# Up products of the third block on half the rows of TensorE, two side by side, with their messages between the halves

## Chip, cores and metric

One core of one Trainium2 chip runs the kernel as one program. The metric is the device time of one execution in microseconds (us); the kernel before takes 377.39 us, the median of three runs (377.11 to 377.71).

## The reference, cut to what matters

Three layers follow each other on 1536 tokens (2 batches of 768) of width 320:

```python
y = attn(q, k, v, i_gate, f_gate, o_gate)        # an mLSTM recurrence, 8 heads of 40, chunked in the kernel
x = y.transpose(0, 2, 1, 3).reshape(1536, 320)
h = maximum(maximum(x @ w1, x @ w2), x @ w3)      # w1, w2, w3: 320 x 768
x = h @ w_out                                     # 768 x 320
h = x @ w_in                                      # 320 x 2048
g = h * tanh(log1p(exp(h)))
out = g @ w_out2                                  # 2048 x 320
```

The change touches the second layer (the three "up" products and their maximum) for the last third of the tokens, the start of the third layer, and one memset of the first.

## The kernel before, in words

**Stages.** The tokens are cut into three blocks of 512. The attention of a block feeds the second layer of that block; when the second layer of the third block (block 2 in the code) is done, the third layer runs over all three blocks, to the end of the span.

**Arithmetic.** Each fp32 operand is split into a high part and a low remainder in a format that TensorE multiplies in one pass (`xh`, `xl`; `hh`, `hl`; `zh`, `zl`; `gh`, `gl`, and weights likewise). A product of width 320 then needs the row groups 0 to 127, 128 to 255 and 256 to 319. For the last 64 rows the high and the low part of the weight lie above each other in one 128-row slot, and the operand's 64 rows stand twice, so that a product on all 128 rows is 8 matmuls (line 570): high by high for three groups, low by high for two, high by low for three.

**The up products before.** `_P(blk, m, i)` makes one product `mm` of 128 columns of w1, w2 or w3 (`i`) by 512 tokens: 8 matmuls of 128 rows, one PSUM bank `m0`, `m1` or `m2` by `i`. There are 6 values of `m`, so 18 products and 144 matmuls in a block. `_Pa` does the first five matmuls of the first product. `_t(blk, m, 0)` copies the first product to SBUF on ScalarE (line 590); `_t(blk, m, 1)` and `_t(blk, m, 2)` take the maximum with the second and the third on VectorE (line 592). `_hh`, `_hl` split the result, and `_d` multiplies it with w_out into banks `m0`, `m1`, `m2`; `_e` and `_ea` empty these (lines 629 to 639).

**The order of the work.** Up to the start of the third layer the order on every engine is written out by hand in the three strings of `PLAN`: `follow` calls the steps in that order, and TensorE, VectorE, ScalarE, GpSimd and SyncE each keep it (`manual_schedule`, line 667). So an instruction that waits holds back what is behind it on its engine. A buffer or bank is given to a new tile when all users of the old one are done. The plan also holds, between the products, the steps that bring weights in: `fet` (a DMA on SyncE's queue), `sc` (two ScalarE passes), `mg` (VectorE), `rd` (ScalarE or VectorE), `cut` (VectorE or GpSimd), and `zh`, `zl`, which split the third layer's input. The third layer keeps an order by hand on TensorE alone, and its first matmuls are put between matmuls of the plan by the scheduler.

**Halves.** The third layer's products already run on 64 rows: `together` (line 705) issues two chains in turn, one on rows 0 to 63 and one on rows 64 to 127, into two banks. A product there is made of 8 matmuls on one half and 7 on the other, since the low weights by the low operand are left out. When one half adds to a bank that the other half wrote, TensorE must know that the writes have landed: `together` puts a no-op on SyncE's queue that waits for the last matmul of the first half (line 713), and the first matmul of the second half waits for it. This is what "message" means below.

**Late fetches.** Five weight tiles of the third layer (`LATE`, lines 790 to 793) are fetched after space of the second layer has come free.

**The startup.** `fe:0` writes rows 0 to 15 of `fzs` (line 207), `clear:2` zeroes all of `fzs` on VectorE after it (line 167), and `fl:0` writes rows 32 to 47 (line 218).

Of the kernel before, what the change touches and what calls it, by code (L numbers as in the profile page):

```python
# [8 lines left out]
F32 = mybir.dt.float32  # L9
# [5 lines left out]
P = 128  # L15
B, H, S, D = 2, 8, 768, 40
# [12 lines left out]
ZAT = (5, 12, 13)  # L29
LATE = {4: "i7", 6: "p4", 8: "p5", 10: "p6", 12: "p7"}  # L30
PLAN = (
# [33 lines left out]
)  # L65
HALF = P // 2
NP = KF2 // 2
# [2 lines left out]
I32 = mybir.dt.int32  # L70
# [4 lines left out]
def mlstm_moe_kernel(ctx, tc, fi0, fir, qk2, q3, nat, w13, wo1, wi2, wo2, ident, bmask, out):  # L75
    nc = tc.nc
# [10 lines left out]
    m1 = pa.enter_context(tc.tile_pool(name="m1", bufs=1))  # L87
# [7 lines left out]
    def bank(tag, name):  # L95
        return (mmp if tag[0] == "m" else pat).tile([P, 512], F32, tag=tag, name=name)
# [30 lines left out]
    m0 = mt0[:, 1:L + 1]  # L127
# [6 lines left out]
    xs = {}  # L134
    act = {}
# [3 lines left out]
    slabs = {}  # L139
# [441 lines left out]
    def _P(blk, m, i):  # L581
        products(blk, m, i, range(5, 8) if m == i == 0 else range(8))

    def top(blk, m):
        return zraw[:, m % 3, blk * XB:(blk + 1) * XB]

# [19 lines left out]
    @step  # L606
    def _d(blk, j, part):
        wo = slabs["o", -1]
        if part == 0:
            downs[blk, j] = bank(f"m{j}", f"mz{blk}_{j}")  # L610
        pv = downs[blk, j]
        for k in range(KF1 - 1) if part == 0 else (KF1 - 1,):
            hh, hl = hs[blk, k]
            if j < 2:
                hi, lo = wo[:, k, j * P:(j + 1) * P], wo[:, k, 384 + j * P:384 + (j + 1) * P]
                nc.tensor.matmul(pv, hi, hh, start=(k == 0), stop=False)  # L616
                nc.tensor.matmul(pv, lo, hh, start=False, stop=False)  # L617
                nc.tensor.matmul(pv, hi, hl, start=False, stop=(k == KF1 - 1))  # L618
            else:
                both = wo[:, k, 256:384]  # L620
                nc.tensor.matmul(pv, both, hh, start=(k == 0), stop=False)  # L621
                nc.tensor.matmul(pv, both, hl, start=False, stop=(k == KF1 - 1))  # L622
# [75 lines left out]
            return outp.tile([P, 512], F32, tag="mx" if p else f"o{i}", name=f"h2_{blk}_{m}")[:, 0:BLOCKS[blk][1]]  # L698
        return bank("m0" if p % 2 else f"m{1 + i}", f"h2_{blk}_{m}")[:, 0:BLOCKS[blk][1]]

    issued = []
    turns = {}
    behind = mybir.DependencyInfo(mybir.DependencyClass.Sync, mybir.DependencyReason.DATA)

    def together(*lanes):
        told = None
        for ops in zip(*lanes):
            for g, (out_, a, r, first, last) in enumerate(ops):
                was = turns.get(out_.tensor.name)
                wait = was and not first and len(lanes) == 2 and was[0] == (2, 1 - g) and not (seen and seen[-1] >= was[1])  # L710
                if wait:
                    seen.append(was[1])
                    told = nc.sync.nop().ins
                    tc.add_manual_dep(told, issued[was[1]].name, behind, reason="the other half of the rows has written the bank")
                mm = nc.tensor.matmul(out_, a, r, start=first, stop=last).ins  # L715
                if wait:
                    tc.add_manual_dep(mm, told.name, behind, reason="the other half of the rows has written the bank")
                turns[out_.tensor.name] = (len(lanes), g), len(issued)
                issued.append(mm)
        return told  # L720

    seen = []

    def lane(ps, w, i, g, zh, zl):
        r = slice(g * HALF, (g + 1) * HALF)
        seq = [(0, zh, 0), (2, zh, 0), (0, zl, 0), (1, zh, 1), (3, zh, 1), (1, zl, 1), (4, zh, 2)]
        if g == i:
            seq.append((4, zl, 2))
        n = len(seq)
        return [(ps, w[r, 2 * j + i], z[r, k], g == i and x == 0, g != i and x == n - 1) for x, (j, z, k) in enumerate(seq)]  # L730

    def expand(blk, p, ps, second):
        w, z = slabs["i", p], zs2[blk]
        if second:
            together(lane(ps[1], w, 1, 0, *z), lane(ps[0], w, 0, 1, *z))
        else:
            together(lane(ps[0], w, 0, 0, *z), lane(ps[1], w, 1, 1, *z))

# [48 lines left out]
    pools["pb2"] = ctx.enter_context(tc.tile_pool(name="pb2", bufs=4, reuse_waits="tile"))  # L787
    pz2 = ctx.enter_context(tc.tile_pool(name="pz2", bufs=1, reuse_waits="tile"))
    st2 = ctx.enter_context(tc.tile_pool(name="st2", bufs=1, reuse_waits="tile"))
    for item in LATE.values():  # L790
        k, g = item[0], int(item[1:])
        spare[k, g] = st2.tile([P, 640, 2], I32, tag=f"r_{item}", name=f"raw_{item}")
        act["fet"](k, g)

    def ahead(blk, m):
        if m in ZAT and blk + 1 < len(BLOCKS):
# [28 lines left out]
    with tc.manual_schedule(engines={ET.PE}):  # L825
        ps0, ps1 = pair_of(0, 0), pair_of(0, 1)
        expand(0, 0, ps0, False)
        expand(0, 1, ps1, False)
        expand(0, 0, ps0, True)
        evict(0, 0, ps0)  # L830
        expand(0, 1, ps1, True)
        evict(0, 1, ps1)
        for q in range(2, NP * len(BLOCKS)):
            turn_of(q)
        for ms in ((KF2 - 4, KF2 - 3), (KF2 - 2, KF2 - 1)):
            for j in range(4):
                for m in ms:
                    together(terms(last, m, j, slice(0, P), False, m == KF2 - 1))
                if KF2 - 1 in ms:
                    write(last, j)  # L840
# [69 lines left out]
```

## Time and profile before

| | us |
|---|---|
| median of three runs | 377.39 |
| the profiled execution | 377.48 |
| span of that execution (first to last instruction) | 375.7 |
| of it, second layer of the third block on TensorE | 159.66 to about 206 |
| of it, the 144 up matmuls of that block | 159.66 to 193.22 |
| of it, third layer | about 206 to 375.7 |

Times in the rows are us from the start of the span. PE is TensorE's matmul, PEld its weight load, DVE VectorE, ACT ScalarE, POOL GpSimd, SP SyncE, SPq its DMA queue. L574 is line 574 of the kernel. A row of the timeline gives start, length, engine, line, operation, output and input with shape, and how many instructions it merges; in brackets how long the engine was idle before and what ended that. A row that merges several back-to-back matmuls is as long as from the first one's start to the last one's end, and the next row can start before that end, since matmuls are pipelined. PEclk in a table of windows is the clock that TensorE was granted, 1.00 for 2.4 GHz and 0.50 for 1.2 GHz.

### The profile page before, as it was taken

How to read it: one execution, taken by the hardware profiler on the slowest of the kernel's cores; microseconds unless marked ns; L12 is line 12 of the kernel's file. 1: busy time of each engine (PE TensorE's matmuls, PEld its weight loads, DVE VectorE, ACT ScalarE, POOL GpSimd, SP SyncE). 2: the span in 40 equal slices, each digit the busy share in tenths (PEclk: the TensorE clock that was granted, in tenths of full speed). 3: DMA queues.
4: the chain of work that ended last, by engine and by line, in shares of the span. 5: the costliest groups of instructions: out<-in, count | busy, mean ns of one | idle time of the engine just before them, and what ended most of it. 6: DMA issues, size and time to landing. Idle time of an engine off the chain costs nothing.

```text
span 375.7 us, 7421 instructions
## 1 busy us (share of the span) xinstructions
PE 367.9 (98%) x2993; PEld 318.9 (85%) x2993; DVE 198.8 (53%) x344; ACT 175.6 (47%) x353; POOL 100.2 (27%) x111
## 2 busy tenths in 40 slices
PE   8899999999999999999999999999999999999996
PEld 4798888888888888888787899988988989989986
DVE  6879999998665854466582654422212112212112
ACT  4867866942521412473734967634334233333231
POOL 5783485665300122221540043330010110000000
PEclk9889999999999999999999999999999999999999
DMA  7876996637591210033420440000200000200001
GB/s 206 273 217 217 354 321 230 210 139 255 182 309 48 91 70 0 2 95 114 142 70 0 165 188 3 3 0 2 72 2 2 0 2 2 72 2 3 0 2 70
DMA packets 15668, 38.80 MB, mean 103 GB/s; under 512 B 1886, under 2 KB 8515, under 8 KB 15635
## 3 DMA queue, kind: packets, MB, share of 16 engines
q1 hardware_dynamic: 15635, 38.34, 30.8%
q8 instruction: 23, 0.38, 0.4%
q14 instruction: 10, 0.08, 0.1%
HBM read 36.29 MB, written 2.04 MB: 102 GB/s over the span
## 4 chain that ended last, share of the span: by engine, by line
PE 93%; DVE 3%; DMA 2%; issue 1%; ACT 1%; SPq 0%; DVEq 0%; ACTq 0%
PE mm L574 25%; PE o L715 23%; PE h L715 22%; PE it L394 6%; PE mz L618 2%; PE mz L616 2%; PE mz L617 2%; PE it L392 2%; PE sc_c L355 2%; PE sp L456 2%; PE mz L621 1%; DMA cp<-dram_c 1%; PE mz L622 1%; PE xp L425 1%; DVE dt L342 1%
## 5 line engine op out<-in xcount | busy, mean ns | idle before, releaser
L744 DVE TENSOR_TENSOR gl<-g,gh 128x512 fp32r<-128x512 f32 x48 | 34.9, 732 | 101.9 <-ACT g L743 101.9
L715 PE MATMUL o<-wo,gh 64*128 64x320 f32 (+1 forms) x736 | 85.0, 306 | 0.0
L715 PE MATMUL h<-zh,wi 64*128 64x512 f32 x480 | 75.2, 390 | 0.0
L574 PE MATMUL mm<-xh,w 128*128 128x512 f32 x270 | 72.0, 396 | 0.0
L715 PEld LDWEIGHTS o<-wo,gh 64*128 64x128 f32 (+1 forms) x736 | 65.0, 185 | 2.2 <-issue 0.4
L742 ACT ACTIVATE gh<-h 128x512 fp32r<-128x512 f32 x48 | 29.0, 604 | 77.7 <-PE h L715 77.6
L715 PE MATMUL o<-wo,gl 64*128 64x320 f32 (+1 forms) x368 | 59.3, 306 | 0.0
L574 PEld LDWEIGHTS mm<-xh,w 128*128 128x128 f32 x270 | 49.4, 188 | 10.7 <-issue 0.4
L715 PEld LDWEIGHTS h<-zh,wi 64*128 64x128 f32 x480 | 44.0, 185 | 9.3 <-ACT zraw L629 0.5
L715 PE MATMUL h<-zl,wi 64*128 64x512 f32 x240 | 47.3, 391 | 0.0
L574 PE MATMUL mm<-xl,w 128*128 128x512 f32 x162 | 45.7, 390 | 0.1
L574 PEld LDWEIGHTS mm<-xl,w 128*128 128x128 f32 x162 | 30.3, 188 | 6.8 <-issue 0.5
L715 PEld LDWEIGHTS o<-wo,gl 64*128 64x128 f32 (+1 forms) x368 | 36.1, 185 | 0.0
L592 DVE TENSOR_TENSOR zraw<-zraw,mm 128x512 f32<-128x512 f32 x36 | 24.6, 683 | 20.7 <-PE mm L574 19.1
L743 ACT ACTIVATE g<-h 128x512 f32<-128x512 f32 x48 | 29.2, 608 | 0.0
L394 PE MATMUL it<-vp,dt 128*128 128x41 f32 x192 | 26.2, 281 | 1.6 <-DVE dt L361 1.6
L715 PEld LDWEIGHTS h<-zl,wi 64*128 64x128 f32 x240 | 22.5, 184 | 5.3 <-issue 0.4
L394 PEld LDWEIGHTS it<-vp,dt 128*128 128x128 f32 x192 | 25.2, 200 | 1.9 <-POOL kp L377 1.7
L654 POOL TENSOR_TENSOR zl<-zraw,zh 128x512 fp32r<-128x512 f32 x9 | 11.6, 1293 | 54.9 <-ACT zh L648 54.8
L602 POOL TENSOR_TENSOR hl<-zraw,hh 128x512 fp32r<-128x512 f32 x11 | 14.7, 1336 | 39.1 <-DVE hh L152 24.1
L590 ACT ACTIVATE zraw<-mm 128x512 f32<-128x512 f32 x18 | 10.7, 592 | 21.8 <-PE mm L574 21.7
L342 DVE TENSOR_TENSOR_SCAN dt<-dt,eye 128x512 f32<-128x512 f32 x16 | 19.1, 1206 | 0.0
(153 smaller groups left out, 524.4 us busy)
## 6 DMA issues: line engine op xcount, KB each, us to landing
na<-in_nat_dram SPq DMA_DIRECT2D x12, 484.0 KB
raw_w<-in_w_dram SPq DMA_DIRECT2D x9, 640.0 KB
raw_i<-in_wi_dram SPq DMA_DIRECT2D x8, 640.0 KB
raw_p<-in_wo_dram SPq DMA_DIRECT2D x8, 640.0 KB
dt<-dram_f SPq DMA_DIRECT2D x8, 512.0 KB
qall<-in_qk_dram SPq DMA_DIRECT2D x24, 160.0 KB
raw_o<-in_wo_dram SPq DMA_DIRECT2D x3, 640.0 KB
out_dram<-ob SPq DMA_DIRECT2D x12, 160.0 KB
```

The lines of the kernel that those rows point to most:

```text
L342: nc.vector.tensor_tensor_scan(half, *((t["fp", j], idr) if ("fp", j) in t else (half, eyes[0])), 0.0, op0=ALU.mult, op1=ALU.add)
L355: nc.tensor.matmul(scs[h % 2][:, (h // 2) * L:(h // 2 + 1) * L], qk[r:r + 64, 1, h // 2], qk[r:r + 64, 0, h // 2], start=True, stop=True)
L394: nc.tensor.matmul(it[:, h], t["dt"][:, h], vps[u % 2][:, h], start=(c == 0), stop=(c == 0 or h == h1 - 1))
L574: nc.tensor.matmul(ups[blk, m, i], *seq[k], start=(k == 0), stop=(k == 7))
L590: nc.scalar.activation(top(blk, m), ups[blk, m, 0], AF.Copy)
L592: nc.vector.tensor_tensor(top(blk, m), top(blk, m), ups[blk, m, i], op=ALU.max)
L602: engine(dve).tensor_tensor(ls, top(blk, m), h.bitcast(F32), op=ALU.subtract)
L654: nc.gpsimd.tensor_tensor(zl[:, j], zraw[:, j, t0:t0 + tb], zh[:, j].bitcast(F32), op=ALU.subtract)
L715: mm = nc.tensor.matmul(out_, a, r, start=first, stop=last).ins
L742: mark[blk, m] = nc.scalar.activation(gh, ps, AF.Mish)
L743: nc.scalar.activation(g, ps, AF.Mish)
L744: low[blk, m] = nc.vector.tensor_tensor(gl, g, gh.bitcast(F32), op=ALU.subtract)
```

## The change

**Up products of block 2 on half the rows.** `_Pa` and the 18 `_P` of block 2 are replaced by nine pairs of products, `q = 2p` and `q = 2p + 1` with `q = 3m + i`. `A:2,p` runs 8 matmuls of product `2p` on rows 0 to 63 together with 8 of product `2p + 1` on rows 64 to 127 (`Aa` is the first five of `A:2,0`); `B:2,p` runs 7 and 7 on the other halves and so completes both products at the same time. The banks go round over four: `m0`, `m1`, `m2` and `o3`, by `q` modulo 4. Each `B` gets one message on SyncE's queue, nine in all. The three down products of block 2 take the banks that follow (`m0`, `m2`, `o3`). The steps of the other engines keep their order; the cut between the second and the third string moves.

**Messages ahead of fetches.** `expand` hands back the last message, and the late fetches are issued on SyncE's queue after the message of `expand(0, 1, ps1, True)`.

**The memset of `fzs`** (`clear:2`) moves from behind `fe:0` to the start of VectorE's queue.

```diff
-    "clear:4 l3:2 clear:1 clear:0 first:0 ... ma:1 fe:0 fill:4@c1 clear:2 "
+    "clear:4 l3:2 clear:1 clear:2 clear:0 first:0 ... ma:1 fe:0 fill:4@c1 "
...
-    "fet:p,0 d:1,1,0 rd:i,0,1,1 rd:i,1,0 rd:i,0,0,1 zh:0,1 cut:i,0,1,1 cut:i,0,0 sc:i,2 d:1,2,1 d:1,1,1 rd:i,1,1 mg:i,2 Pa:2 e:1,1 cut:i,1,0,1 fet:p,1 "
-    "e:1,2 P:2,0,0 rd:i,2,1,1 cut:i,1,1 P:2,0,1 zh:0,2 ea:1 rd:i,2,0 t:2,0,0 P:2,0,2 sc:i,3 t:2,0,1 cut:i,2,0,1 cut:i,2,1,1 P:2,1,0 t:2,0,2 mg:i,3 P:2,1,1 "
-    "rd:i,3,1,1 t:2,1,0 fet:p,2 cut:i,3,1 sc:p,0 P:2,1,2 t:2,1,1 rd:i,3,0,1 cut:i,3,0,1 P:2,2,0 t:2,1,2 sc:p,1 mg:p,0 hh:2,0,1 P:2,2,1 rd:p,0,0 fet:i,4 "
-    "hl:2,0 t:2,2,0 P:2,2,2 t:2,2,1 cut:p,0,0,1 P:2,3,0 t:2,2,2 mg:p,1 P:2,3,1 rd:p,1,0 fet:i,5 zh:0,0 cut:p,1,0,1 hh:2,1 P:2,3,2 t:2,3,0 hl:2,1 sc:p,2 "
-    "t:2,3,1 zl:0,1 P:2,4,0 t:2,3,2 sc:i,4 mg:p,2 P:2,4,1 hh:2,2 zl:0,2 fet:p,3 rd:p,2,0 t:2,4,0 hl:2,2,1 P:2,4,2 t:2,4,1 cut:p,2,0 P:2,5,0 t:2,4,2 sc:i,5 "
-    "hh:2,4,1 mg:i,4 P:2,5,1 t:2,5,0 hl:2,4,1 fet:i,6 rd:i,4,0 hh:2,3,1 hl:2,3,1 rd:i,4,1 P:2,5,2",
+    "fet:p,0 d:1,1,0 rd:i,0,1,1 rd:i,1,0 rd:i,0,0,1 zh:0,1 cut:i,0,1,1 cut:i,0,0 sc:i,2 d:1,2,1 d:1,1,1 rd:i,1,1 mg:i,2 Aa:2 A:2,0 A:2,1 B:2,0 B:2,1 e:1,1 "
+    "cut:i,1,0,1 fet:p,1 e:1,2 rd:i,2,1,1 cut:i,1,1 zh:0,2 ea:1 rd:i,2,0 t:2,0,0 sc:i,3 t:2,0,1 A:2,2 cut:i,2,0,1 cut:i,2,1,1 t:2,0,2 mg:i,3 rd:i,3,1,1 "
+    "t:2,1,0 A:2,3 B:2,2 B:2,3 fet:p,2 cut:i,3,1 sc:p,0 t:2,1,1 rd:i,3,0,1 cut:i,3,0,1 t:2,1,2 A:2,4 sc:p,1 mg:p,0 hh:2,0,1 rd:p,0,0 fet:i,4 hl:2,0 t:2,2,0 "
+    "t:2,2,1 A:2,5 B:2,4 B:2,5 cut:p,0,0,1 t:2,2,2 mg:p,1 rd:p,1,0 fet:i,5 zh:0,0 cut:p,1,0,1 hh:2,1 t:2,3,0 A:2,6 hl:2,1 sc:p,2 t:2,3,1 zl:0,1 t:2,3,2 "
+    "A:2,7 B:2,6 sc:i,4 mg:p,2 hh:2,2 zl:0,2 fet:p,3 rd:p,2,0 t:2,4,0 hl:2,2,1 t:2,4,1 A:2,8 B:2,7 B:2,8",
...
+    def tile_of(n, name):
+        return outp.tile([P, 512], F32, tag="o3", name=name) if n % 4 == 3 else bank(f"m{n % 4}", name)
+
+    def rows(blk, q, g, ks):
+        xh, xl = xs[blk]
+        w, i = slabs["w", q // 2], q % 2
+        r = slice(g * HALF, (g + 1) * HALF)
+        seq = [(0, xh, 0), (1, xh, 1), (4, xh, 2), (2, xh, 0), (3, xh, 1), (0, xl, 0), (1, xl, 1)]
+        if g == i:
+            seq.append((4, xl, 2))
+        m = divmod(q, 3)
+        if g == i and 0 in ks:
+            ups[blk, m[0], m[1]] = tile_of(q, f"mm{blk}_{m[0]}_{m[1]}")
+        n = len(seq)
+        return [(ups[blk, m[0], m[1]], w[r, 2 * j + i], x[r, k], g == i and z == 0, g != i and z == n - 1) for z, (j, x, k) in enumerate(seq) if z in ks]
+
+    @step
+    def _Aa(blk):
+        together(rows(blk, 0, 0, range(5)), rows(blk, 1, 1, range(5)))
+
+    @step
+    def _A(blk, p):
+        ks = range(8) if p else range(5, 8)
+        together(rows(blk, 2 * p, 0, ks), rows(blk, 2 * p + 1, 1, ks))
+
+    @step
+    def _B(blk, p):
+        together(rows(blk, 2 * p + 1, 0, range(8)), rows(blk, 2 * p, 1, range(8)))
...
-            downs[blk, j] = bank(f"m{j}", f"mz{blk}_{j}")
+            downs[blk, j] = tile_of(18 + (2, 0, 1)[j], f"mz{blk}_{j}") if blk == 2 else bank(f"m{j}", f"mz{blk}_{j}")
...
-            together(lane(ps[1], w, 1, 0, *z), lane(ps[0], w, 0, 1, *z))
+            return together(lane(ps[1], w, 1, 0, *z), lane(ps[0], w, 0, 1, *z))
...
-    for item in LATE.values():
-        k, g = item[0], int(item[1:])
-        spare[k, g] = st2.tile([P, 640, 2], I32, tag=f"r_{item}", name=f"raw_{item}")
-        act["fet"](k, g)
+
+    def fetch_late():
+        for item in LATE.values():
+            k, g = item[0], int(item[1:])
+            spare[k, g] = st2.tile([P, 640, 2], I32, tag=f"r_{item}", name=f"raw_{item}")
+            act["fet"](k, g)
...
-        expand(0, 1, ps1, True)
+        told = expand(0, 1, ps1, True)
+        with tc.issue_after(told):
+            fetch_late()
```

## Rows read from the trace of the kernel before

**Rows 1.** The page's head: span, and TensorE's busy time.

```profile
span 375.7 us, 7421 instructions
...
PE 367.9 (98%) x2993; PEld 318.9 (85%) x2993; DVE 198.8 (53%) x344; ACT 175.6 (47%) x353; POOL 100.2 (27%) x111
```

**Rows 2.** Timeline of PE in the third block's up products (start, us).

```profile
159.66 1.29 PE L574 MATMUL mm<-xh,w 128*128 128x512 f32 x5
...
161.47 1.30 PE L574 MATMUL mm<-xh,w 128*128 128x512 f32 x5
...
180.74 0.84 PE L574 MATMUL mm<-xl,w 128*128 128x512 f32 x3
181.51 0.73 PE L715 MATMUL h<-zh,wi 64*128 64x512 f32 x4
182.17 1.44 PE L574 MATMUL mm<-xh,w 128*128 128x512 f32 x5
...
193.22 0.39 PE L616 MATMUL mz<-hh,wo 128*128 128x512 f32 x1
```

**Rows 3.** The chain that ended last, in the third layer (start, us, what).

```profile
216.94 3.42 PE h L715 x30
```

**Rows 4.** The tile mm in this block: weight loads, ns min/median/max.

```profile
L574 PEld LDWEIGHTS mm<-xh,w x90: 186/188/189, 159.4 to 192.1; 128*128 128x128 f32 x90
```

**Rows 5.** Timeline of ACT beside these products.

```profile
159.86 0.60 ACT L629 ACTIVATE zraw<-mz 128x512 f32<-128x512 f32 x1 [0.70 <-PE mz L618]
...
167.11 0.60 ACT L590 ACTIVATE zraw<-mm 128x512 f32<-128x512 f32 x1 [2.43 <-PE mm L574]
...
172.84 0.58 ACT L590 ACTIVATE zraw<-mm 128x512 f32<-128x512 f32 x1
177.64 0.74 ACT L154 ACTIVATE wo<-dec_p 128x640 fp32r<-128x640 f32 x1 [4.22 <-DVE dec_p L505]
178.28 0.62 ACT L648 ACTIVATE zh<-zraw 128x512 fp32r<-128x512 f32 x1
178.80 0.62 ACT L154 ACTIVATE hh<-zraw 128x512 fp32r<-128x512 f32 x1
179.32 0.58 ACT L590 ACTIVATE zraw<-mm 128x512 f32<-128x512 f32 x1
```

**Rows 6.** Timeline of DVE beside these products.

```profile
161.71 0.69 DVE L639 TENSOR_TENSOR zraw<-sw,mz 128x512 f32<-128x512 f32 x1 [0.64 <-ACT sw L633]
...
169.00 0.69 DVE L592 TENSOR_TENSOR zraw<-zraw,mm 128x512 f32<-128x512 f32 x1 [1.55 <-PE mm L574]
...
170.74 0.69 DVE L592 TENSOR_TENSOR zraw<-zraw,mm 128x512 f32<-128x512 f32 x1
...
176.18 0.69 DVE L592 TENSOR_TENSOR zraw<-zraw,mm 128x512 f32<-128x512 f32 x1 [0.32 <-PE mm L574]
```

**Rows 7.** SyncE's queue, lines 713 and 490: count, ns, first and last start.

```profile
L713 SPq EVENT_SEMAPHORE  x2: 17/17/17, 206.3 to 208.5; - x2
...
L490 SPq DMA_DIRECT2D raw_p<-in_wo_dram x4: 423/430/590, 211.1 to 212.7; - x4
```

**Rows 8.** Timelines of DVE and ACT in the startup.

```profile
5.79 0.17 DVE L167 MEMSET fzs<- 128x128 f32 x1 [0.44 <-ACT fzs L207]
...
13.58 0.69 DVE L361 TENSOR_TENSOR dt<-sc_m,dt 128x512 f32<-128x512 f32 x1
...
10.18 0.80 ACT L499 ACTIVATE dec_w<-raw_w 128x640 f32<-128x640 f32 x1 [0.81 <-DMA raw_w<-in_w_dram]
...
13.35 0.20 ACT L154 ACTIVATE dl<-dt 128x8 f32<-128x8 f32 x1
```

**Rows 9.** Windows: length, busy us (count) of PE, PEld, DVE, ACT, POOL; PEclk; DMA; GB/s.

```profile
15.45:22.28 6.83, 6.83 (x36) 6.61 (x37) 4.86 (x9) 3.35 (x8) 5.60 (x8) 0.50 0.96 251
13.45:15.02 1.57, 0.00 (x1) 0.04 (x1) 1.55 (x4) 1.47 (x6) 1.40 (x2) 1.00 0.77 263
...
78.18:78.91 0.73, 0.00 (x0) 0.03 (x1) 0.73 (x2) 0.00 (x0) 0.73 (x2) 1.00 0.00 0
```

More of the change, by code (lines that the diff above doesn't have):

```diff
@@ L582, in _P, with together @@
         products(blk, m, i, range(5, 8) if m == i == 0 else range(8))
+    issued = []
+    turns = {}
+    behind = mybir.DependencyInfo(mybir.DependencyClass.Sync, mybir.DependencyReason.DATA)
+    def together(*lanes):
+        told = None
+        for ops in zip(*lanes):
+            for g, (out_, a, r, first, last) in enumerate(ops):
+                was = turns.get(out_.tensor.name)
+                wait = was and not first and len(lanes) == 2 and was[0] == (2, 1 - g) and not (seen and seen[-1] >= was[1])
+                if wait:
+                    seen.append(was[1])
+                    told = nc.sync.nop().ins
+                    tc.add_manual_dep(told, issued[was[1]].name, behind, reason="the other half of the rows has written the bank")
+                mm = nc.tensor.matmul(out_, a, r, start=first, stop=last).ins
+                if wait:
+                    tc.add_manual_dep(mm, told.name, behind, reason="the other half of the rows has written the bank")
+                turns[out_.tensor.name] = (len(lanes), g), len(issued)
+                issued.append(mm)
+        return told
+    seen = []
+    def tile_of(n, name):
[22 more added lines that the diff above has]
+        together(rows(blk, 2 * p + 1, 0, range(8)), rows(blk, 2 * p, 1, range(8)))
     def top(blk, m):
@@ L699, in hbank @@
         return bank("m0" if p % 2 else f"m{1 + i}", f"h2_{blk}_{m}")[:, 0:BLOCKS[blk][1]]
[L701 to L722, printed above, removed]
     def lane(ps, w, i, g, zh, zl):
```

7 rows, old and new, of the table PLAN are left out of this document.

## The prediction, made before the changed kernel ran

> **What bounds the kernel now.** The page's head comes first: TensorE is busy for 367.9 of 375.7 us [rows 1], so only what shortens its row of matmuls, or makes it wait, can show in the total. The timeline of PE in the changed stage comes next: from 159.66 to 193.22 us one product follows the other without a gap, and the one break is an insertion of third-layer matmuls at 181.51 [rows 2]. The timelines of ACT and DVE in the same stretch say when banks are emptied; both engines wait for PE there [rows 5, 6], so in the kernel before the emptying is never late. The profiled execution took 377.48 us, 0.09 over the median of 377.39; the sum is made against it. A measurement of this kernel can tell about 0.2% (0.75 us) from no change.
>
> **Matmuls removed.** Eight full-row matmuls lie between 159.66 and 161.47, 0.2265 us each [rows 2]. In the third layer 30 matmuls of 64 rows, 15 pairs, take 3.42 us, 0.228 a pair [rows 3]. So a pair costs what one full-row matmul costs, and side by side gains nothing by itself. What is saved is the low by low part: nine pairs of products at 8 + 7 steps are 135 steps in place of 144. Nine steps less are **-2.05 us**.
>
> The rule that speaks for more: the Trainium skill's page TensorE: Matmul & The Clock Gate (Part 3, The mechanism) says that a weight load overlaps a running matmul only if the two are on different groups of rows; by it the 144 full-row matmuls would each carry their load bare, and halves could hide it. The rows differ: a load takes 188 ns [rows 4] inside a spacing of 226.5 ns [rows 2], and a matmul that had to wait for it would be spaced by more than 188 ns plus its own 512 columns. The sum goes by the rows.
>
> **Turns between 128 and 64 rows.** The inserted h matmuls should have come at 180.74 + 3 x 0.2265 = 181.42 and came at 181.51; their two pairs take 0.46, to 181.97, and the next full-row matmul came at 182.17 [rows 2]. So a turn costs 0.09 in and 0.20 out. In the new stage such an insertion needs no turn (-0.29); the stage itself has one in, which falls into the first wait below, and one out (+0.20). Together **-0.09**. The two pairs can run in a wait of PE, since their input is split (`zh:0,0`) inside the longest one below: **-0.46**.
>
> **Waits for banks, the term that decides.** Before, a product took one bank at a time, and its predecessor in that bank had been done for two products. Now `B` completes two products at once, and the next `A` into those banks needs both emptied, while the other engines keep the order they had for products that come one by one. What covers the emptying is one `B` of the other pair, 7 x 0.2265 = 1.59 us. A product can be read 0.20 us (ACT) or 0.28 us (DVE) after its last step: the fourth product's steps end at 159.66 + 4 x 1.813 = 166.91 and ACT starts at 167.11; the fifth's at 168.72 and DVE at 169.00 [rows 2, 5, 6]. A signal between engines takes 0.03 (ACT's 13.55 to DVE's 13.58 [rows 8]); for one to PE I take 0.05. One by one:
> - Entry. `Aa` writes m0 and m1, but m1 holds the down product that `e:1,1` copies at 159.86 to 160.46 [rows 5]. Pairs start at 160.51 in place of 159.75: **0.76**. `A:2,1` (at 162.32) needs m2, read by `ea:1` until 162.40 [rows 6]: **0.13**.
> - `A:2,2` needs an ACT copy and a DVE maximum: 0.20 + 0.60 + 0.03 + 0.69 + 0.05 = 1.57 against 1.59: none, with no margin. `A:2,3` and `A:2,7` have an `A` of 1.81 as more cover: none.
> - `A:2,4` needs `t:2,1,1` and `t:2,1,2`, with a cast and a subtraction between them in DVE's order: 169.00 to 171.43 [rows 6], 2.43; with 0.28 and 0.05 it is 2.76 - 1.59 = **1.17**.
> - `A:2,5` needs `t:2,2,0`, which is behind DVE's merge and ACT's rounding of a weight: from the start of `t:2,1,2` at 170.74 [rows 6] to 173.42 [rows 5] are 2.68, then a maximum: 3.45. `A:2,4` uses 0.74 + 1.81 = 2.55 of it: **0.90**.
> - `A:2,6` needs `t:2,2,2` and `t:2,3,0`. Between them ACT's order has a rounding that waits for a merge behind `t:2,2,2`, then `zh:0,0`, then `hh:2,1`: from 176.18 [rows 6] to 179.90 [rows 5] are 3.72. With 0.28 and 0.05, less 1.59: **2.46**.
> - `A:2,8` stands directly behind `B:2,6`, whose two products it must see emptied, so nothing covers it: 0.20 + 0.58 + 0.03 + 0.69 + 0.05 = **1.55**.
>
> Together 6.97. The down products start behind two `B` and find their banks and operands ready; `t:2,4,2` has 1.59 for 0.97.
>
> **Messages.** Nine no-ops join SyncE's queue, and no row here shows what one costs PE when it is late: from 0 to, say, the 0.20 of a read after a product, so 0 to 1.8 for nine. I take 0, since every `B` stands a whole `A` or `B` (1.59 at least) behind the `A` that it waits for. What is moved on that queue: `fet:p,1` to `fet:i,6` now stand behind messages. `fet:p,1` goes out at the end of `A:2,1`, near 164.3 in place of 159.6, and is first read near 174. The other way round, the message of `B:2,6` is behind `fet:i,5`, which waits for a merge; that merge is done inside the wait of `A:2,6`, long before `B:2,6`.
>
> **Fetches behind messages.** In the trace the two messages are at 206.3 and 208.5 and the late fetches from 210.8 to 212.7 [rows 7]: they stand in that order already. This part does nothing: 0.
>
> **The memset.** It starts at 5.79 after 0.44 of waiting for ACT and holds up DVE's queue [rows 8]. What ends the startup's chain is the multiplication at 13.58, which begins as ACT's copy of `dl` ends at 13.35 + 0.20; that copy hangs on a weight that lands at 10.18 [rows 8]. So 0 is taken; the bounds are -0.44, if that chain moves too, and +0.17, the memset's length ahead of the warm-up matmuls.
>
> **Sum.** -2.05 - 0.09 - 0.46 + 6.97 = +4.37: 381.85 for the profiled execution, 381.8 beside the median.
>
> **Rivals.**
> - *The banks come free in time* (faster). If the emptying takes at most its 1.59 everywhere, only -2.05 - 0.09 is left: 375.2. It decides at 1.59 per pair of banks. For it: the two engines have idle time before (2.43 us ahead of one copy [rows 5]). Against it: the chains of 2.43 and 3.72 us are orders, not load, and `A:2,8` has no cover. If just the entry and `A:2,8` wait, it is -2.05 - 0.09 - 0.46 + 2.31 = -0.29: 377.1, no change.
> - *Waits drop the clock* (slower still). After 1.57 us without a matmul the granted clock fell to 0.50, that is 1.2 GHz, for 6.83 us; after 0.73 it stayed at 2.4 GHz [rows 9]. The waits of 2.46 (2.0 with the inserted pairs) and 1.55 lie about there. At half the clock 6.83 us do 3.4 us of work: at most +3.4, at least about half of that, since a slower PE also waits less: 383.5 to 385.2. Against it: only one fall is seen, and dense matmuls stand around these waits. The Trainium skill's page TensorE: Matmul & The Clock Gate (Part 1) says that an idle engine is put back to half its rate; the trace agrees with its one fall.
> - *Part of the waits goes* because ACT and DVE, held up at one wait, come to the next with less behind them: half of the three middle waits (4.53) away gives 379.6.
> - *The weight loads were bare*: 144 x 0.188 = 27 us less, about 348. Only the page's rule above stands for it; [rows 2, 4] exclude it but for a misreading.
> - *The change does less than it says*: true of the fetches, and already in the sum.
>
> **How the numbers follow.** Waits as worked out: 0.60, with 380.6 to 383.0 as its own range (0.2 us on each of six waits). Clock falls: 0.20. Part of the waits goes, 378.4 to 380.6: 0.09. No change: 0.04. Banks free in time: 0.06. Bare loads: 0.01. So faster 0.07, same 0.04, slower 0.89. The range leaves out the two on the fast side and the ends: 379.4 to 385.2. It holds the bounds of the messages and the memset around the likeliest.
>
> **What would show it.** In the profile after: `mm` written by the helper `together` in forms of 64 rows, a step every 0.228 us; PE idle ahead of six `A`, released by ACT and DVE lines of `_t` (and once by `_e`), the longest near 183 us; up products of some 37.9 us in place of 33.56; late fetches still behind their messages; the third layer as long as before. The sum is wrong if those idle stretches are absent or under 2.6 in total (then no slower), if PE waits for SyncE ahead of a `B`, or if PEclk reads 0.50 anywhere after 23 us.

## The result, and the profile after

The changed kernel takes **382.38 us** (median; 380.68 to 383.51), the kernel before beside it 377.39 (377.11 to 379.11): a ratio of **1.0134 [1.0101, 1.0167]**, 5.0 us slower. The profiled execution took 383.51, with a span of 381.7. It was measured again later, beside other variants (the repeat's profile fell in a disturbed execution and is not read).

> The changed kernel as it is, beside the other variants of this chip job. Theory: 382.4 by its five runs, and the stage from its first up product to the third layer's first o product 58.5 to 58.6 as in its first profile, whatever the startup does. If the startup of the first profile (stage begun at 160.71 in place of 159.66) was that execution's own, the stage begins here anywhere from 158.2 to 160.7, as it did in the first four experiments.

The repeat took 381.55 us, a ratio of 1.0108 [1.0073, 1.0143]: the same loss within the intervals. How much the startup moves is seen from the other profiles instead: the third block's first up product starts anywhere from 158.24 to 160.80.

The head of the page, to be held beside [rows 1]: TensorE is busy for 1.7 us more in a span 6.0 longer, so most of the time was lost in waiting, not in work.

```profile
span 381.7 us, 7676 instructions
...
PE 369.6 (97%) x3119; PEld 318.3 (83%) x3119; DVE 200.2 (52%) x344; ACT 176.1 (46%) x353; POOL 101.3 (27%) x111
```

The timeline of PE in the changed stage, which answers to [rows 2] (columns as there): the first step, every row ahead of which PE waited, the last rows of `B:2,6` (191.71) and of `B:2,8` (198.50), the first down product, and the third layer's first `o` product.

```profile
160.80 0.50 PE L598 MATMUL mm<-xh,w 64*128 64x512 f32 x1
161.56 1.20 PE L598 MATMUL mm<-xh,w 64*128 64x512 f32 x8 [0.26 <-ACT zraw L681]
...
175.68 0.39 PE L598 MATMUL mm<-xh,w 64*128 64x512 f32 x1
176.77 1.42 PE L598 MATMUL mm<-xh,w 64*128 64x512 f32 x9 [0.70 <-DVE zraw L644]
...
179.57 1.19 PE L598 MATMUL mm<-xh,w 64*128 64x512 f32 x8 [0.23 <-DVE zraw L644]
...
186.06 0.73 PE L598 MATMUL h<-zh,wi 64*128 64x512 f32 x4 [1.22 <-ACT zh L700]
187.07 1.40 PE L598 MATMUL mm<-xh,w 64*128 64x512 f32 x9 [0.27 <-ACT zraw L642]
...
191.71 0.83 PE L598 MATMUL mm<-xl,w 64*128 64x512 f32 x4
193.29 0.49 PE L598 MATMUL mm<-xh,w 64*128 64x512 f32 x1 [0.75 <-ACT zraw L642]
194.01 1.44 PE L598 MATMUL mm<-xh,w 64*128 64x512 f32 x9 [0.23 <-DVE zraw L644]
...
198.50 0.83 PE L598 MATMUL mm<-xl,w 64*128 64x512 f32 x4
199.26 0.50 PE L668 MATMUL mz<-hh,wo 128*128 128x512 f32 x1
...
202.36 0.50 PE L670 MATMUL mz<-hl,wo 128*128 128x512 f32 x1 [0.29 <-DVE hl L654]
...
219.27 0.46 PE L598 MATMUL o<-wo,gh 64*128 64x320 f32 x4
```

A bracket counts only the time after the modelled end of the matmul before, so it is shorter than the delay. The delay is read from starts: the first matmul's partner on the other half should have come with it at 160.80; it came at 161.56, 0.76 late. From the first up product to the first down product it takes 38.46 us where it took 33.56 [rows 2]; from there to the first `o` product 20.01, where it was 20.03. So 4.90 us were lost in the up products, and 4.88 on the way to the first `o`. The remaining 1.1 of the 6.0 had been lost before 160.80; the first experiment asks whether the memset did that.

The windows around the longest waits (columns as in [rows 9]) show TensorE's clock at its upper level; from 160.80 to 182.00 it reads 1.00 as well:

```profile
182.00:194.00 12.00, 9.54 (x76) 6.94 (x72) 6.96 (x8) 7.50 (x13) 6.36 (x4) 1.00 0.32 110
194.00:206.00 12.00, 11.70 (x70) 9.06 (x71) 7.98 (x13) 3.56 (x8) 3.27 (x3) 1.00 0.18 56
```

### The profile page after: what moved, and what is told of

Its sections match the earlier page's. It is cut to its first block, busy times and chain, and to the rows that moved or that the text cites. A ratio compares the mean times of both kernels' runs of the same rounds, so it can differ in the third digit from the quotient of the medians.

```text
span 381.7 us, 7676 instructions
## 1 busy us (share of the span) xinstructions
PE 369.6 (97%) x3119; PEld 318.3 (83%) x3119; DVE 200.2 (52%) x344; ACT 176.1 (46%) x353; POOL 101.3 (27%) x111
## 4 chain that ended last, share of the span: by engine, by line
PE 81%; DVE 6%; DMA 5%; ACT 4%; issue 2%; SPq 1%; POOL 0%; DVEq 0%; ACTq 0%
PE o L598 22%; PE h L598 22%; PE mm L574 12%; PE mm L598 5%; PE it L394 5%; PE mz L670 2%; DMA raw_o<-in_wo_dram 2%; PE mz L668 2%; PE mz L669 2%; DMA raw_w<-in_w_dram 2%; PE it L392 2%; PE sc_c L355 2%; PE sp L456 2%; DMA cp<-dram_c 1%; PE mz L673 1%
## 5 line engine op out<-in xcount | busy, mean ns | idle before, releaser
L574 PE MATMUL mm<-xh,w 128*128 128x512 f32 x180 | 48.6, 399 | 0.0
L574 PEld LDWEIGHTS mm<-xh,w 128*128 128x128 f32 x180 | 32.6, 188 | 6.9
L574 PE MATMUL mm<-xl,w 128*128 128x512 f32 x108 | 30.5, 391 | 0.1
L598 PE MATMUL mm<-xh,w 64*128 64x512 f32 x180 | 28.0, 398 | 2.4 <-DVE zraw L644 1.2
L706 POOL TENSOR_TENSOR zl<-zraw,zh 128x512 fp32r<-128x512 f32 x9 | 12.6, 1410 | 54.9 <-ACT zh L700 54.8
L598 PEld LDWEIGHTS mm<-xh,w 64*128 64x128 f32 x180 | 18.7, 184 | 8.7 <-DVE zraw L644 2.5
L574 PEld LDWEIGHTS mm<-xl,w 128*128 128x128 f32 x108 | 20.2, 188 | 4.7 <-issue 0.5
```

What stands on the lines that cost most here:

```text
L574: nc.tensor.matmul(ups[blk, m, i], *seq[k], start=(k == 0), stop=(k == 7))
L706: nc.gpsimd.tensor_tensor(zl[:, j], zraw[:, j, t0:t0 + tb], zh[:, j].bitcast(F32), op=ALU.subtract)
```

## The experiments

In the table a stretch counts from the start of the first up product of the third block; the expectations count from 160.71, where that product would have come without the turn, so that their 4.97 is 4.88 here. Ratios are to the kernel before, run on the same chip.

From the first `o` to the end every profile here has 162.4 us left, so what a variant costs by itself is its last column less 53.59. The second column carries the startup too, which scatters: the kernel before takes 375.7 to 376.7 us in executions with a mean granted clock of 0.994 or 0.995, and 377.2 to 378.3 in those with 0.989 to 0.991. A difference of up to 1.5 us between medians of few runs can come from that alone; the last section shows where it arises.

| kernel | us | ratio [95%] | to the first down product | to the first `o` |
|---|---|---|---|---|
| before | 377.39 | 1 | 33.56 | 53.59 |
| changed | 382.38 | 1.0134 [1.0101, 1.0167] | 38.46 | 58.47 |
| e1, memset and fetches alone | 377.43 | 1.0013 [0.9985, 1.0040] | 33.56 | 53.59 |
| e2, halves alone | 384.78 | 1.0216 [1.0186, 1.0245] | 38.50 | 61.71 |
| e3, emptying first | 378.50 | 1.0046 [1.0025, 1.0066] | 35.49 | 55.50 |
| e4, six banks | 375.99 | 0.9975 [0.9954, 0.9997] | 31.60 | 52.03 |
| e5, six banks, emptying first | 374.67 | 0.9927 [0.9899, 0.9955] | 31.33 | 50.87 |
| e8, e5 and early low parts | 373.90 | 0.9909 [0.9880, 0.9939] | 31.33 | 50.75 |
| e7, each B behind its A | 379.60 | 1.0078 [1.0050, 1.0106] | 36.62 | 56.04 |
| e6, last A later | 380.67 | 1.0109 [1.0072, 1.0145] | 37.28 | 56.68 |
| e9, e8 without the fetch edit | 380.78 | 1.0117 [1.0081, 1.0154] | 31.34 | 56.85 |

**e1: the change without its halves.**

```diff
-    "clear:4 l3:2 clear:1 clear:0 first:0 ... ma:1 fe:0 fill:4@c1 clear:2 "
+    "clear:4 l3:2 clear:1 clear:2 clear:0 first:0 ... ma:1 fe:0 fill:4@c1 "
-        expand(0, 1, ps1, True)
+        told = expand(0, 1, ps1, True)
+        with tc.issue_after(told):
+            fetch_late()
```

> The stage of the kernel before (18 products, no halves), with the two other parts of the change: the memset of fzs at the start of VectorE's queue, the late fetches behind the message. Theory (the loss is bank waits of the halved stage): as before, 377.4 within 0.2%. Rival (the startup loses by the memset): the stage of block 2 began 1.05 us later in the profiled run of after, with a granted clock that rose at 6.40 in place of 5.21; if the memset ahead of the warm-up matmuls is the cause, this kernel takes 378.0 to 378.6, and its stage begins near 160.7; if that was one execution's scatter, the start lies near 159.7 or scatters as much from run to run. Fetches: 0 either way, they stand behind the two messages in both traces.

Neither part changes the time by itself. The first up product starts at 159.63, as before (159.66), with the memset where the change puts it:

```profile
0.89 0.17 DVE L167 MEMSET fzs<- 128x128 f32 x1
...
159.63 1.30 PE L574 MATMUL mm<-xh,w 128*128 128x512 f32 x5
```

So the later start in the changed kernel's profile is not the memset's, but scatter of the startup. The late fetches go out at 210.75 in place of 210.77.

**e2: the halves alone.** The changed kernel with the memset and the fetches put back.

```diff
-    "clear:4 l3:2 clear:1 clear:2 clear:0 first:0 ... ma:1 fe:0 fill:4@c1 "
+    "clear:4 l3:2 clear:1 clear:0 first:0 ... ma:1 fe:0 fill:4@c1 clear:2 "
...
+    fetch_late()
...
-        told = expand(0, 1, ps1, True)
-        with tc.issue_after(told):
-            fetch_late()
+        expand(0, 1, ps1, True)
```

> The halves of block 2 alone: the memset and the late fetches stand as in the kernel before. Theory: the whole loss of the stage, so 381.8 (+4.4) by the sum, 382.4 (+5.0) by the trace of after, where the stretch from the first up product to the third layer's first matmul grew by 4.97; waits of PE of .76 at the entry, 1.1 at A:2,4, 1.0 at A:2,5, 2.4 (with the inserted pairs) at A:2,6, 1.8 at A:2,8. Rival (startup): about 1 us less than after, 381.3, with the stage's start near 159.7.

Both missed: it is slower than the whole change, by 2.4 us between the medians and by 3.24 in the stretch to the first `o` (61.71 and 58.47). The up products are as long (38.50); what is longer comes after them. Timeline of PE, then SyncE's lines 490 and 596 from 196 to 222 us (count, ns, first and last start):

```profile
213.23 0.39 PE L598 MATMUL h<-zh,wi 64*128 64x512 f32 x2
216.53 0.73 PE L598 MATMUL h<-zh,wi 64*128 64x512 f32 x4 [2.91 <-SPq L596]
```

```profile
L490 SPq DMA_DIRECT2D raw_p<-in_wo_dram x4: 425/514/654, 214.2 to 215.8; - x4
...
L490 SPq DMA_DIRECT2D raw_i<-in_wi_dram x2: 327/328/328, 197.3 to 213.8; - x2
L596 SPq EVENT_SEMAPHORE  x3: 17/17/17, 210.3 to 221.1; - x3
```

Five late fetches go out from 213.8 on; the last begins at 215.8, and one takes up to 0.65 us to issue. The message for which PE waits stands behind them, and PE goes on at 216.53. In the kernel before both messages were out, at 206.3 and 208.5, ahead of the fetches [rows 7]; with the halves only one is (210.3). So the fetch edit gains nothing on its own (e1) and about 3 us next to the halves. Why the order turns over was not traced: the third layer's steps on SyncE's queue aren't written out by hand.

**e3: four banks, the emptying ahead of the weight steps.**

```diff
-    ... t:2,1,1 rd:i,3,0,1 cut:i,3,0,1 t:2,1,2 A:2,4 sc:p,1 mg:p,0 hh:2,0,1 rd:p,0,0 fet:i,4 hl:2,0 t:2,2,0 t:2,2,1 A:2,5 ...
-    ... t:2,2,2 mg:p,1 rd:p,1,0 fet:i,5 zh:0,0 cut:p,1,0,1 hh:2,1 t:2,3,0 A:2,6 ...
+    ... t:2,1,1 t:2,1,2 A:2,4 rd:i,3,0,1 cut:i,3,0,1 t:2,2,0 t:2,2,1 A:2,5 ... sc:p,1 mg:p,0 hh:2,0,1 rd:p,0,0 fet:i,4 hl:2,0 ...
+    ... t:2,2,2 t:2,3,0 A:2,6 mg:p,1 rd:p,1,0 fet:i,5 zh:0,0 cut:p,1,0,1 hh:2,1 ...
```

> The changed kernel with only the order of the emptying steps altered: t:2,1,2 ahead of rd:i,3,0,1; t:2,2,0 and t:2,2,1 ahead of sc:p,1; t:2,3,0 ahead of mg:p,1. The same matmuls, banks, messages. Theory (the waits are the order on ScalarE and VectorE, as the sum had it): the waits ahead of A:2,4, A:2,5 and A:2,6 go; those of the entry (.76) and A:2,8 (about 1.6 to 1.8) stay, and a new one of about 1.3 us comes ahead of A:2,7, whose bank is emptied by a step that now stands behind the weight steps: 3.06 us less than after, so 379.3. Rival (ScalarE and VectorE have too much to do beside shorter products, so that any order is late): the waits move and their sum stays, within 0.5 us of after. Rival (halves themselves cost, by messages or pairs): no change either, with PE idle in rows that name SyncE or with pairs longer than .228 us.

The stretch is 2.97 us shorter than the changed kernel's; 3.06 was expected. The three middle waits are gone, the entry and `A:2,8` remain, and a new one stands ahead of `A:2,7`. Timeline of PE, the rows with a wait:

```profile
158.99 1.20 PE L598 MATMUL mm<-xh,w 64*128 64x512 f32 x8 [0.26 <-ACT zraw L681]
...
183.32 1.42 PE L598 MATMUL mm<-xh,w 64*128 64x512 f32 x9 [0.22 <-DVE zraw L644]
...
188.50 1.42 PE L598 MATMUL mm<-xh,w 64*128 64x512 f32 x9 [0.23 <-DVE zraw L644]
```

ScalarE and VectorE do the same work in both, with the same matmuls and banks, so the middle waits came from the order in which they did it.

**e4: six banks in rotation.**

```diff
-        return outp.tile([P, 512], F32, tag="o3", name=name) if n % 4 == 3 else bank(f"m{n % 4}", name)
+        tag = ("m0", "o3", "o2", "mx", "m1", "m2")[n % 6]
+        return bank(tag, name) if tag[1] in "012" and tag[0] == "m" else outp.tile([P, 512], F32, tag=tag, name=name)
...
-            downs[blk, j] = tile_of(18 + (2, 0, 1)[j], f"mz{blk}_{j}") if blk == 2 else bank(f"m{j}", f"mz{blk}_{j}")
+            downs[blk, j] = tile_of((0, 1, 2)[j], f"mz{blk}_{j}") if blk == 2 else bank(f"m{j}", f"mz{blk}_{j}")
...
-    ... Aa:2 A:2,0 A:2,1 B:2,0 B:2,1 ... A:2,2 ... A:2,3 B:2,2 B:2,3 ...
+    ... Aa:2 A:2,0 A:2,1 B:2,0 A:2,2 B:2,1 ... A:2,3 B:2,2 ... A:2,4 B:2,3 ...
```

> The changed kernel with six banks in rotation (m0, o3, o2, mx, m1, m2) in place of four, and an order on TensorE in which each A stands ahead of the B of the pair before it (A:2,1 B:2,0 A:2,2 B:2,1 and so on, the last B by itself); the steps of the other engines in the order of the change. Theory (banks come free too late for four in rotation): every wait but one of about .7 ahead of A:2,7 goes, the nine steps saved are seen, about 6.3 us less than after: 376.1, and about 1 us under before. Rival (messages cost): each B still stands a whole A behind its message's matmul, so a loss that stays here with PE idle ahead of a B belongs to the messages. Rival (order of the emptying decides, not the number of banks): the waits ahead of A:2,4 to A:2,6 stay in part, 378 to 380.

376.0, as expected: most of the nine saved steps is seen (31.60, which is 1.96 under the kernel before). Two things change at once here, the number of banks and the order of `A` and `B` on TensorE, and no run parts them. Of the wait expected at `A:2,7` little is left: ScalarE's copy ends at 182.62 and the second half of `A:2,7` starts at 182.67, but two pairs of the third layer (at 182.07) fill most of the gap. The only wait that a row names is the one for a low part, at the down products:

```profile
194.39 0.50 PE L672 MATMUL mz<-hl,wo 128*128 128x512 f32 x1 [0.29 <-DVE hl L656]
```

**e5: six banks and `t:2,3,0` ahead of `mg:p,1`.**

```diff
-    ... t:2,2,2 mg:p,1 rd:p,1,0 fet:i,5 zh:0,0 cut:p,1,0,1 hh:2,1 t:2,3,0 A:2,7 B:2,6 hl:2,1 ...
+    ... t:2,2,2 t:2,3,0 A:2,7 B:2,6 mg:p,1 rd:p,1,0 fet:i,5 zh:0,0 cut:p,1,0,1 hh:2,1 hl:2,1 ...
```

> Six banks in rotation as in the last experiment, and t:2,3,0 ahead of mg:p,1 and the steps behind it. Theory (bank waits are all that the halves cost): no wait of PE for the emptying lines is left, only the one for hl at the down products; .7 us less than with six banks alone where that had a wait at A:2,7, but its trace showed none there, so between 0 and .7 less: 375.3 to 376.0, 1.4 to 2.0 under before. Rival (no more to gain; the order only moves work of VectorE and ScalarE): as with six banks alone, 376.0, or later weights for the third layer, up to 376.5.

374.67, below the range of either. The up products gain 0.27, the wait for `hl` is gone too, and the pair of the third layer that stood among e4's down products (at 201.42, with a turn each way) now comes behind them, so 1.16 is gained up to the first `o`. This is the halved stage without a wait; PE's timeline shows an `A` of 1.82 us (161.50 to 163.32) and a `B` of 1.59 (163.32 to 164.91) back to back:

```profile
161.50 1.31 PE L599 MATMUL mm<-xh,w 64*128 64x512 f32 x10
...
163.32 1.30 PE L599 MATMUL mm<-xh,w 64*128 64x512 f32 x10
164.45 0.62 PE L599 MATMUL mm<-xl,w 64*128 64x512 f32 x4
164.91 1.30 PE L599 MATMUL mm<-xh,w 64*128 64x512 f32 x10
...
190.87 0.50 PE L670 MATMUL mz<-hh,wo 128*128 128x512 f32 x1
```

**e8: the low parts earlier.**

```diff
-    ... hl:2,2,1 t:2,4,1 cut:p,2,0 t:2,4,2 sc:i,5 hh:2,4,1 mg:i,4 t:2,5,0 hl:2,4,1 fet:i,6 rd:i,4,0 hh:2,3,1 hl:2,3,1 ...
+    ... hl:2,2,1 t:2,4,1 hh:2,3,1 hl:2,3,1 cut:p,2,0 t:2,4,2 sc:i,5 hh:2,4,1 mg:i,4 t:2,5,0 hl:2,4,1 fet:i,6 rd:i,4,0 ...
```

> The last kernel with hh:2,3,1 and hl:2,3,1 moved from behind rd:i,4,0 to behind t:2,4,1, into idle time of VectorE (2.02 us ahead of t:2,4,2 in the six-bank trace). In the trace of after the first down product waits .29 for that hl, and its subtraction takes 1.67 us beside a cut and zl on GpSimd in place of .69. Theory (the low part stands too late in VectorE's order): the wait goes, the stretch to the third layer's first o product is .3 to .45 shorter: 375.0 to 375.6. Rival (another low part, hl:2,4,1, is late next): nothing gained, PE waits for hl at a later matmul of the down product.

What the theory wanted to remove was gone in e5 already; the stretch is 0.12 shorter, and 373.90 against 374.67 can't be told apart (the ratios' intervals overlap). It is the fastest of all, 3.4 us under the kernel before by the ratio and 2.84 by the stretch.

**e7: each `B` directly behind its `A`.**

```diff
-    ... Aa:2 A:2,0 A:2,1 B:2,0 B:2,1 ... A:2,2 ... A:2,3 B:2,2 B:2,3 ...
+    ... Aa:2 A:2,0 B:2,0 A:2,1 B:2,1 ... A:2,2 B:2,2 ... A:2,3 B:2,3 ...
```

> The changed kernel with each B directly behind its A, four banks, the others' order as it is: now all nine messages stand behind the matmul that they report, with nothing to cover them, and each pair of banks has a whole A and B more to be emptied in. Theory (a message costs PE something only where nothing covers it; the bank waits shrink with the cover): PE waits nine times for SyncE ahead of a B; at .2 us each that is +1.8, while the waits ahead of A:2,4 to A:2,8 shrink; together 380.8 to 382.0. At .4 us each no change against after. Rival (messages are free even uncovered): 379 and no row that names SyncE; rival (a late message costs over .5 us): slower than after, 383 and more.

The time (379.6, some 2 us less than the changed kernel's) is under the theory's range and looks like the rival's "messages are free", yet its rows say otherwise. PE's timeline of two pairs and around the wait for `zh`, and what SyncE's line 596 held up:

```profile
162.99 1.31 PE L598 MATMUL mm<-xh,w 64*128 64x512 f32 x10
164.12 0.85 PE L598 MATMUL mm<-xl,w 64*128 64x512 f32 x6
165.07 1.43 PE L598 MATMUL mm<-xh,w 64*128 64x512 f32 x10
...
166.79 1.30 PE L598 MATMUL mm<-xh,w 64*128 64x512 f32 x10
...
178.22 1.31 PE L598 MATMUL mm<-xh,w 64*128 64x512 f32 x10
...
181.22 0.74 PE L598 MATMUL h<-zh,wi 64*128 64x512 f32 x4 [1.01 <-ACT zh L700]
...
183.41 1.30 PE L598 MATMUL mm<-xh,w 64*128 64x512 f32 x10
```

```profile
L596 SPq EVENT_SEMAPHORE  x9: 17/17/17, 161.2 to 193.1; - x9
...
  PEld mm L598: 4.2, 8
```

From `A` (162.99) to `B` (165.07) are 2.08 us in place of 1.82, and from there to the next `A` 1.72 in place of 1.59: an uncovered message costs 0.26 + 0.13 = **0.39 us**. Eight are waited for (the ninth falls into the wait for `zh`), 3.1 in all. The table of waits by PE doesn't name SyncE, since in its own row only 0.10 us lie between the modelled end of one matmul (164.12 + 0.85) and the start of the next; its weight loads (PEld) carry the wait. What made the kernel faster is that of the bank waits only the entry's is left. The pair with the wait for `zh` takes 5.19 (178.22 to 183.41) where 1.82 + 1.59 and 0.46 for the two inserted pairs would do, so 1.32 more: 31.33 + 0.76 + 1.32 + 3.1 = 36.5, measured 36.62.

**e6: `A:2,8` behind `B:2,7`.**

```diff
-    A:2,7 B:2,6 sc:i,4 mg:p,2 ... t:2,4,1 A:2,8 B:2,7 B:2,8
+    A:2,7 B:2,6 B:2,7 sc:i,4 mg:p,2 ... t:2,4,1 A:2,8 B:2,8
```

> The changed kernel with A:2,8 behind B:2,7 in place of ahead of it. B:2,7 then fills 1.59 us of the time in which the banks of A:2,8 are emptied, and the message for B:2,8 stands directly behind A:2,8, uncovered. Theory (the wait of 1.84 ahead of A:2,8 is the lack of any cover, and an uncovered message costs the .39 a pair that nine of them showed with each B behind its A): the wait falls to about .25 and one message adds .39, so the stretch from the first up product to the first down product is about 1.2 us shorter than the 38.4 to 38.6 of the changed kernel, and the time 381.2 beside 382.4. Rival (another cause of that wait, as the weight steps on ScalarE behind B:2,6): the wait stays above 1 us.

The up products are 1.18 shorter (37.28), as the theory had it. In PE's timeline no row ahead of `A:2,8` names a wait; from `A:2,8` (192.90) to `B:2,8` (195.36) are 2.46 us in place of 1.82, which is the rest of the bank wait and the message together. By the time alone nothing is shown: the ratio of 1.0109 lies beside 1.0134 and 1.0108 of the changed kernel.

```profile
192.90 1.69 PE L598 MATMUL mm<-xh,w 64*128 64x512 f32 x10
...
195.36 1.42 PE L598 MATMUL mm<-xh,w 64*128 64x512 f32 x10
```

**e9: the fastest kernel without the fetch edit.**

```diff
+    fetch_late()
...
-        told = expand(0, 1, ps1, True)
-        with tc.issue_after(told):
-            fetch_late()
+        expand(0, 1, ps1, True)
```

> The kernel with six banks and the early low part, with the late fetches taken out from behind the message, as in the kernel before. Theory (beside the halves the fetches get ahead of a message that PE needs, as in the variant with the halves alone, where PE waited 2.91 us for SyncE at 216.5): the wait of about 3 us is back near the start of the third layer, 376.5 to 377.0. Rival (it was the late stage of that variant that brought it, so it goes where the stage is short): no wait for SyncE, 373.9 as with the fetches behind the message.

The wait is back, also where the stage is short, so the rival is out. But it costs 6.1 us in the stretch to the first `o` (6.9 between the medians), not 3. PE's timeline, then windows (columns as in [rows 9]):

```profile
210.36 1.22 PE L599 MATMUL h<-zh,wi 64*128 64x512 f32 x4 [3.00 <-SPq L597]
```

```profile
207.36:209.50 2.14, 0.00 (x0) 0.00 (x0) 2.03 (x6) 2.06 (x4) 0.00 (x0) 1.00 0.45 86
209.50:210.36 0.86, 0.00 (x0) 0.00 (x0) 0.69 (x1) 0.00 (x0) 0.00 (x0) 0.54 0.93 351
210.36:216.40 6.04, 6.04 (x28) 4.82 (x30) 1.24 (x2) 2.64 (x6) 0.00 (x0) 0.50 1.02 410
216.40:219.00 2.60, 2.60 (x36) 2.50 (x36) 1.80 (x3) 0.85 (x3) 0.00 (x0) 1.00 0.32 128
```

In the course of the wait the granted clock falls to its lower level and stays there to about 216.4: 6 us of matmuls at half the clock, so 3 more are lost. The stretch is 6.10 longer than e8's: 3.0 of waiting and 3.1 of slow matmuls. In e2 a wait of 2.91 left the clock at 1.00.

## Why the prediction was right, and where it was not

**The sum.** 381.8 was forecast, 382.38 measured; +4.37 by the sum, 4.97 by the profile when the stretch is counted from 160.71, where the first up product would have come without the turn. Of the 0.60 between them, 0.09 is an oversight of the sum: it lets the turn into 64 rows fall into the entry's wait, but counts that wait from 159.75, which is already behind the turn. The waits make 0.35 of it and the end of the stage 0.11 (both below). The forecast rested on bank waits, and e3 shows that cause by itself: with nothing changed but the emptying's order 3 us of them go. In e5, with six banks and both orders changed, they are gone, and nothing else in the halved stage costs time.

**Steps saved.** -2.05 and -0.09 for turns; the stage without waits (e5) takes 31.33 in place of 33.56, so -2.23. The rule of the Trainium skill's page TensorE: Matmul & The Clock Gate (Part 3, The mechanism), that a weight load overlaps only matmuls on other groups of rows (the section's text names a background weight buffer beside them), would have made halves worth far more; the runs don't show that, the measured gain is that of the removed steps.

**The waits**, by starts in the timeline of PE above and the rows between:

| ahead of | forecast | measured |
|---|---|---|
| entry | 0.76 | 0.76 (161.56 - 160.80) |
| A:2,1 | 0.13 | 0.12 |
| A:2,3 | 0 | 0.13 |
| A:2,4 | 1.17 | 1.09 (176.77 - 175.68) |
| A:2,5 | 0.90 | 0.98 (179.57 - 176.77 - 8 steps) |
| A:2,6 | 2.46 | 2.40 (187.07 - 184.67) |
| A:2,8 | 1.55 | 1.84 (194.01 - 192.17) |
| sum | 6.97 | 7.32 |

The one wait that was clearly mis-sized is `A:2,8`. ScalarE's copy starts 0.47 after the slot of the last step should have ended (192.17), where 0.20 was taken from full-row products; the copy (0.60) is as long as forecast. The two chains no longer ran in step there: the last four matmuls of `B:2,6` take 0.83 (191.71), where four in step take 0.62 (e5, 164.45), so the last one came about a step (0.21) late, and the copy began 0.26 behind it. Timeline of ACT:

```profile
192.64 0.60 ACT L642 ACTIVATE zraw<-mm 128x512 f32<-128x512 f32 x1 [1.75 <-PE mm L598]
```

The two pairs of the third layer did run inside the longest wait (186.06), as the -0.46 had it. The end of the stage cost 0.31 for the 0.20 taken (the slot of the last step should end at 198.95, and the down product starts at 199.26), and the same late chain is in it: the row at 198.50 takes 0.83 as well, so some 0.1 of the 0.31 is left for the turn. The rows with a wait do not hold all: 135 steps, 7.32 and 0.31 make 38.2 of the 38.46 us.

After the up products, "find their ... operands ready" was wrong once: a low part is late (202.36, 0.45 by starts). It costs nothing net, since the stretch to the first `o` is as long as before; there the remaining pairs of the third layer come behind all down products, where in the kernel before one of them stood among these, so a turn each way is saved.

**Messages.** 0 was right for this order: no row of PE or of its loads waits for SyncE. The upper bound of 0.20 each was not: uncovered, one costs 0.39 (e7).

**Fetches.** "They stand in that order already. This part does nothing: 0" is the step that failed. It read an order of the kernel before, which holds without the halves (e1) and not with them (e2, e9). That the total was not hurt is luck: the halves turn the order over, and the edit, brought together with them, turns it back. Left out, it would have cost 3.24 us by the stretch (e2), and 6.1 in the fastest version (e9).

**The memset.** 0, within the interval of e1.

**Rivals.** "The banks come free in time" gave 375.2; e5, where they do, takes 374.67. "Waits drop the clock" did not happen in the stage; its price shows in e9. (Its sign, a clock of 0.50 after 23 us, is met by the letter: the startup's own fall lasts from 16.64 to 23.47 in this profile, which runs some 1.2 us later than that of the kernel before. No wait of the stage is behind it.) "Part of the waits goes" did not: the middle waits come to 4.47, forecast 4.53.

## What to carry to other kernels

When two tiles are completed by one instruction stream side by side, count banks for two tiles being filled, two being emptied and two ahead, and look at the order of the engines that empty them before looking at their load: here four banks lost 5 us, and six, with the emptying and the order of `A` and `B` changed too, won about 3, with the same matmuls (five were not tried). With four banks what covered the messages left the banks bare, and the other way round: each `B` directly behind its `A` took away the middle bank waits and cost 3.1 us of messages (e7). The Trainium skill's page TensorEngine Tiling (Array Packing), section Restrictions and Gotchas, warns that tiling by rows raises the pressure on PSUM since the tiles write to different banks; the runs agree: 7.3 us of waits with four banks, none in e5 with six. An order on a queue that nobody wrote down is no property to rely on: a part of a change that "does nothing" in the kernel before may be what keeps another part from costing 3 to 6 us.

## What the runs showed of the hardware beyond that

- **The clock after a wait.** In e9 it fell some 2.2 us into the wait of 3.00; in the kernel before it fell at 15.45, 0.4 us behind the end of a wait of 1.57 [rows 9]; in e2 it did not fall in or after a wait of 2.91. So the length of the wait alone doesn't decide. The time at the lower level differs too: in the startup it was 6.83 us before [rows 9], while in e3 the windows 15 to 18 and 18 to 21 us read 0.72 and 0.71 and the next 1.00, that is 3.4 us in all. There the third block starts 1.4 us earlier (158.24). At half the clock 3.4 us less are some 1.7 us of work, an estimate from these windows, and that is about the distance between the two groups of times that the kernel before has in the section on the experiments.

```profile
15.00:18.00 3.00, 3.00 (x22) 3.00 (x21) 2.88 (x7) 2.91 (x6) 2.77 (x6) 0.72 0.93 264
18.00:21.00 3.00, 3.00 (x28) 2.88 (x27) 2.15 (x3) 0.98 (x6) 1.96 (x3) 0.71 0.82 217
21.00:24.00 3.00, 3.00 (x33) 2.71 (x32) 2.08 (x6) 2.97 (x8) 1.98 (x3) 1.00 0.97 267
```

- **VectorE beside GpSimd.** The low part that PE waited for at 202.36 took 1.67 us where the one before it took 0.68; while it ran, GpSimd ran two subtractions, the first of them begun 0.23 earlier. In the kernel before the same low part met the same subtraction the other way round: VectorE began first and took 0.69, and GpSimd's took 1.69 in place of 1.35. DVE, then POOL, of the changed kernel, then one row of each of the kernel before:

```profile
199.58 0.68 DVE L654 TENSOR_TENSOR hl<-zraw,hh 128x512 fp32r<-128x512 f32 x1
...
200.64 1.67 DVE L654 TENSOR_TENSOR hl<-zraw,hh 128x512 fp32r<-128x512 f32 x1
```

```profile
200.41 1.35 POOL L545 TENSOR_TENSOR wi<-dec_i,wi 128x512 fp32r<-128x512 f32 x1 [7.44 <-ACT wi L154]
201.71 1.74 POOL L706 TENSOR_TENSOR zl<-zraw,zh 128x512 fp32r<-128x512 f32 x1
```

```profile
190.84 0.69 DVE L602 TENSOR_TENSOR hl<-zraw,hh 128x512 fp32r<-128x512 f32 x1
...
190.98 1.69 POOL L545 TENSOR_TENSOR wi<-dec_i,wi 128x512 fp32r<-128x512 f32 x1 [4.58 <-ACT wi L154]
```

The Trainium skill's page GPSIMD Engine Reference (1. Specifications) says that GpSimd shares its SBUF interfaces with VectorE, with contention for VectorE instructions that have two SBUF inputs; this one reads two SBUF tiles, and the rows agree: of the two, the one that began later was the longer for it.
